# A planned first stage on one core: scores on eight small array tiles, values times rows on two row tiles, and the weight conversion's clip and low word on another engine

## The chip, the cores and the metric

The kernel runs on one core of one Trainium2 chip. The core has a matmul engine (PE, with its weight loads shown as PEld), a vector engine (DVE), an activation engine (ACT), a general engine (POOL) and a queue engine that issues transfers (SP). The metric is device microseconds of one execution; lower is better.

## The reference, cut to what matters

Three blocks follow one another. The first is an attention over a small memory: the rows of `phi` (32 memory slots) are turned into weights `a`, keys and values are pooled with them, and each query attends to the 32 pooled keys.

```python
a = exp(phi - max(phi, axis=2)); a = a / (sum(a, axis=2) + 1e-9)   # b h s m, m = 32
k_m = einsum('bhsm,bhsd->bhmd', a, k); v_m = einsum('bhsm,bhsd->bhmd', a, v)
scores = (1 / sqrt(64)) * q @ k_m.T                                # b h s m
attn = softmax(scores); attn_out = attn @ v_m                      # b h s d
x = attn_out.transpose(0, 2, 1, 3).reshape(8, 576, 512)
h = relu(x.T @ w_tok1) @ w_tok2; u = x + h.T                       # mixes the 576 tokens
x = u + relu(u @ w_ch1) @ w_ch2                                    # 1536 hidden channels
```

The third block is a causal attention with four experts and a top-2 gate. Batch is 8, heads 8, sequence 576, head dimension 64. The weights of the token and channel blocks come as float64.

## The kernel before

Accuracy comes from splitting operands into a high part in a one-pass format (F32R) and a low remainder; a product of two such pairs is three matmuls (`mm3`, L199). Plain F32 matmuls stand in the trace as two records each.

The kernel has three stages. The first, which all of the change is in, goes through 16 units; a unit is one batch and four of its heads (`units`, L296). Unit `n` runs `front(n)` (softmax of `phi` over the sequence, pooled keys and values, queries transposed), `rows(n)` (scores, softmax over the 32 slots, and the weights turned over) and `mix(n)` (token mixing; its output `u1` goes to HBM). After every second unit two `block(j)` do a part of the channel block (two of its 12 slices of 128 hidden channels) on half a batch each; the last two blocks run after the stage. The stage also turns float64 weights into pairs of F32R words (`convert`, L736): ACT takes the absolute high word (`c_abs`), POOL clips it (`c_clip`, L751), POOL scales the low word (`c_low`, L755), DVE joins them and sets the sign (L759, L762), ACT writes the high part (L767), and the remainder is taken on DVE for weights that are needed at once and on POOL for the ten pieces that are needed after the stage (`c_lo`, L771). There are 19 pieces: five for the token weights, four for the blocks of the stage, and ten with a due time (`chan(i, fc, 90000 + 20000 * c)`, L849).

The order of all instructions of the stage is computed in Python before the kernel is built: every step is handed to a planner (`Plan`, L63) with its engine, an assumed duration in ns, what it reads and writes, and the buffer pool it takes from; `order()` lists the steps engine by engine as the assumed durations let them start, the most urgent first. Each engine then executes its list strictly in that order. The assumed durations of the two POOL steps of a conversion are

```python
add("POOL", 150 + 600 * x, c_clip, ...)                     # x = columns / 512
y = add("POOL", 150 + 600 * x, c_low, ..., take="cy", ...)
```

The scores of a unit are four F32 matmuls with a contraction of 64 (the keys of a pair of heads are held block-wise with zeros, so K is 128 and M is 64), on the left and the right half of the array's columns (L481); two pairs of heads, each with 512 and 64 queries. Values times rows (L608 to L610) contract over the 128 rows of four heads with a masked value tile, three matmuls of 288 columns for each of two channel groups and two halves of the sequence. PSUM has two banks each for `t`, `g`, `s` and `b`.

Of the kernel before, what the change touches and what calls it, by code (L numbers as in the profile page):

```python
# [62 lines left out]
class Plan:  # L63
# [5 lines left out]
    def add(self, eng, ns, fn, reads=(), writes=(), take=None, due=None):  # L69
        t = dict(i=len(self.tasks), eng=eng, ns=ns, fn=fn, take=take, due=due, pre=set(), gives=[], holders=0)  # L70
# [19 lines left out]
    def order(self):  # L90
# [13 lines left out]
        slots = dict(self.pools)  # L104
# [9 lines left out]
        while len(out) < len(ts):  # L114
            for eng, cand in open_.items():
                if free_at[eng] > now:
                    continue
                can = [i for i in cand if ready_at[i] <= now and (ts[i]["take"] is None or slots[ts[i]["take"]] > 0)]
# [7 lines left out]
                if t["take"] is not None:  # L126
                    slots[t["take"]] -= 1
# [13 lines left out]
            while True:  # L141
                if i >= 0:
# [5 lines left out]
                    for o in ts[i]["gives"]:  # L148
                        o["holders"] -= 1
                        if not o["holders"]:  # L150
                            slots[o["take"]] += 1
# [8 lines left out]
def fused_kernel(ctx: ExitStack, tc, q, k, v, phi, w_tok1, w_tok2, w_ch1, w_ch2,  # L160
# [106 lines left out]
    with ExitStack() as sa:  # L267
# [12 lines left out]
        kmask = wa.tile([128, 2, 64], F32, name="kmask")  # L280
        DVE.memset(vmask[:], 0.0)
        DVE.memset(kmask[:], 0.0)
        for h in range(4):
            DVE.memset(vmask[32 * h:32 * h + 32, h, :], 1.0)
            DVE.memset(kmask[32 * h:32 * h + 32, h % 2, :], 1.0)
        NB2 = 2
        phb = [ld.tile([128, 4, 5, M], F32, name=f"phb{i}") for i in range(NB2)]
        qTb = [ld.tile([128, 2, S], F32, name=f"qTb{i}") for i in range(NB2)]
# [3 lines left out]
        qn_ = ld.tile([128, 5, 4, D], F32, name="qn")  # L292
        DVE.memset(kv_[ST:128, :, :, 4, :], 0.0)
        DVE.memset(qn_[ST:128, 4, :, :], 0.0)
# [10 lines left out]
        def psum(name, shape=(128, 512)):  # L305
            return pp.tile(list(shape), F32, name=name, bufs=1 if name == "s" else 2)

        def loads(n):
# [15 lines left out]
            def l_q():  # L324
                src = q[b, hs]
                for j in range(4):
                    SP.dma_start(qn_[:, j, :, :], src[:, 0:SM, :].rearrange("h (p j) d -> p j h d", j=4)[:, j])
                SP.dma_start(qn_[0:ST, 4, :, :], src[:, SM:S, :].rearrange("h p d -> p h d"))
# [4 lines left out]
                        q=lambda: add("SP", (3000, 3200), l_q, writes=["qn"]))  # L333

        def front(n):
# [5 lines left out]
            def top():  # L341
                mx = st["mx"] = wk_.tile([128, 4, M], F32, name="pmx", bufs=1)
                m2 = wk_.tile([128, 4, 2, M], F32, name="pm2", bufs=1)
# [50 lines left out]
            def k_scale():  # L394
# [3 lines left out]
                DVE.reciprocal(r[:], r[:])  # L398
                ks = st["ks"] = wk_.tile([128, 2, 64], F32, name="ks", bufs=1)
                DVE.scalar_tensor_tensor(ks[:], p[:, None, 0:64].to_broadcast([128, 2, 64]), r[:],  # L400
                                         kmask[:], op0=OP.mult, op1=OP.mult)
# [24 lines left out]
            def q_t(i):  # L426
                if i < 2:
                    st["q", i] = psum("t")
                    for j in range(4):
                        PE.transpose(st["q", i][:, 128 * j:128 * j + 128], qn_[:, j, 2 * i:2 * i + 2, :], ident[:])  # L430
                    return
                st["q", 2] = psum("t", (128, 2, 128))
                for pr in range(2):
                    PE.transpose(st["q", 2][:, pr, :], qn_[:, 4, 2 * pr:2 * pr + 2, :], ident[:])

            def q_c(i):
                if i < 2:
                    ACT.activation(qT[:, i, 0:512].rearrange("k (p j) -> k p j", j=4),
                                   st["q", i][:].rearrange("k (j p) -> k p j", j=4), AF.Copy)
                else:  # L440
                    ACT.activation(qT[:, :, 512:S], st["q", 2][:, :, 0:ST], AF.Copy)

            add("DVE", 950, top, reads=[kph], writes=["mx"])
# [12 lines left out]
            c = add("DVE", 640, k_scale, reads=[(n, "g")], writes=["ks", (n, "r")])  # L456
# [6 lines left out]
            add("POOL", 780, lambda: v_mask("vh", "Vh"), reads=["vh"], writes=[("Vh", n % 3)])  # L463
            add("POOL", 780, lambda: v_mask("vl", "Vl"), reads=["vl"], writes=[("Vl", n % 3)])
            for i in range(3):
                a = add("PE", (4, 4, 2)[i] * TR, lambda i=i: q_t(i), reads=["qn"], writes=[(n, "q", i)], take="t")
# [3 lines left out]
        def rows(n):  # L470
# [4 lines left out]
            def score():  # L475
                p = st["s"] = psum("s", (128, S))
# [7 lines left out]
            def turn():  # L484
                st["x"] = wk_.tile([128, NB, M], F32, name="ssb", bufs=1)
                DVE.transpose(st["x"][:].rearrange("p k m -> p (k m)"), st["s"][:])
# [1156 lines left out]
```

## Time and profile before

| | us |
|---|---|
| median of three runs | 1269.46 (1268.49 to 1270.68) |
| the profiled execution, its own time | 1271.36 |
| its span in the profile | 1269.6 |
| PE busy | 1186.2 (93%) |
| DVE / ACT / POOL busy | 803.8 / 603.7 / 518.5 |

Line numbers are those of the kernel before. "Busy" of a group is the time in which at least one of its instructions ran; the mean is that of one instruction. Matmuls are pipelined, so the start-to-start distance of neighbours says what one costs, and its record is longer. "Idle before" names what ended the engine's wait. PEclk is the granted clock as a share of full speed.

### The profile page before, as it was taken

Reading aid. Unit: us, or ns where it says so; the run is one execution under the profiler, and the core shown is the slowest. Engines: PE = TensorE matmul, PEld = TensorE weight load, DVE = VectorE, ACT = ScalarE, POOL = GpSimd, SP = SyncE. Lnnn points to the kernel's source line nnn. Section 1 sums busy time; section 2 is a strip of 40 time slices with the busy share of each in tenths; the row PEclk is TensorE's granted clock in tenths of the full one; section 3 lists DMA queues with packets and bytes.
Section 4 is the critical chain, followed back from the end, with each engine's and each line's share of the span. In section 5 each row is a group of like instructions: output and inputs, shape, how many; then the busy total and the mean of one; then the engine's idle time right before and its main releaser. Section 6 shows DMA issues by size and latency. Waiting matters only on the chain.

```text
span 1269.6 us, 23616 instructions
## 1 busy us (share of the span) xinstructions
PE 1186.2 (93%) x8578; PEld 1088.5 (86%) x8578; DVE 803.8 (63%) x1991; ACT 603.7 (48%) x1575; POOL 518.5 (41%) x630
## 2 busy tenths in 40 slices
PE   5567789999997999999999999999999999999998
PEld 3456678899996888998999988999999999999986
DVE  5677776766447175566756552487767677776763
ACT  2344445444434132322232211477776776776775
POOL 5789973434300021211221043564636365373421
PEclk9887999999998999999999999999999999999999
DMA  9666666565226122023212233422332333323523
GB/s 228 181 184 182 179 177 193 161 172 154 75 102 233 47 100 67 34 67 100 100 34 67 100 109 110 131 83 77 95 87 80 89 102 86 94 69 80 158 74 108
DMA packets 161171, 145.07 MB, mean 114 GB/s; under 512 B 73248, under 2 KB 128800, under 8 KB 161056
## 3 DMA queue, kind: packets, MB, share of 16 engines
q1 hardware_dynamic: 161056, 143.57, 38.2%
q8 instruction: 68, 1.11, 0.4%
q14 instruction: 47, 0.39, 0.1%
HBM read 91.10 MB, written 40.89 MB: 104 GB/s over the span
## 4 chain that ended last, share of the span: by engine, by line
PE 77%; POOL 7%; DVE 7%; issue 3%; ACT 3%; DMA 2%; SPq 1%; DVEq 0%; ACTq 0%; POOLq 0%
PE g L199 21%; PE o L199 15%; PE h L199 14%; PE y L1415 4%; PE b L669 3%; PE b L199 3%; PE s L1306 3%; PE t L1370 2%; POOL cy L755 2%; POOL cm L751 1%; PE s L1328 1%; PE s L481 1%; PE g L612 1%; PE g L613 1%; DMA ub<-u_d 1%
## 5 line engine op out<-in xcount | busy, mean ns | idle before, releaser
L1351 POOL TENSOR_TENSOR a<-a,cf 128x128 f32<-128x128 f32 (+3 forms) x128 | 88.2, 720 | 68.1 <-DVE cf L1343 62.1
L199 PE MATMUL o<-hh,w2h 128*128 128x512 f32 x288 | 109.5, 395 | 3.8 <-ACT hh L915 3.8
L199 PE MATMUL o<-hl,w2h 128*128 128x512 f32 x288 | 112.8, 392 | 0.1
L199 PE MATMUL o<-hh,w2l 128*128 128x512 f32 x288 | 112.4, 390 | 0.0
L923 ACT ACTIVATE hh<-m 128x256 fp32r<-128x256 f32 x96 | 38.9, 415 | 111.1 <-DVE m L994 71.4
L1295 DVE CUSTOM_DVE_ANT_0 ssb<-s,cmask 128x128 f32<-128x128 f32 (+2 forms) x144 | 68.5, 482 | 26.7 <-PE s L1306 18.0
L1308 ACT ACTIVATE a<-ssb,nb 128x128 f32<-128x128 f32 (+3 forms) x128 | 71.4, 558 | 18.0 <-DVE nb L1295 15.0
L971 POOL TENSOR_TENSOR tl<-ub,th 128x512 fp32r<-128x512 f32 x12 | 18.1, 1525 | 136.3 <-ACT th L970 136.3
L956 POOL TENSOR_TENSOR ub<-ub 128x512 f32<-128x512 f32 x6 | 9.8, 1630 | 150.4 <-DVE ul L206 150.4
L924 DVE SCALAR_TENSOR_TENSOR hl<-m,hh 128x256 fp32r<-128x256 f32 x96 | 58.2, 615 | 17.6 <-ACT hh L923 15.5
L1207 POOL TENSOR_TENSOR xl<-p,xh 128x288 fp32r<-128x288 f32 x60 | 47.4, 809 | 52.6 <-ACT xh L1206 52.3
L199 PE MATMUL h<-uh,w1h 128*128 128x512 f32 (+2 forms) x200 | 66.4, 334 | 2.0 <-ACT uh L203 2.0
L199 PEld LDWEIGHTS o<-hh,w2h 128*128 128x128 f32 x288 | 54.4, 190 | 14.3 <-ACT hh L915 4.1
L199 PE MATMUL h<-uh,w1l 128*128 128x512 f32 (+2 forms) x200 | 66.7, 334 | 0.0
L199 PE MATMUL h<-ul,w1h 128*128 128x512 f32 (+2 forms) x200 | 65.9, 334 | 0.0
L199 PE MATMUL g<-xh,qkh 128*128 128x288 f32 x232 | 65.3, 301 | 0.0
L199 PE MATMUL g<-xh,qkl 128*128 128x288 f32 x232 | 63.9, 296 | 0.0
L199 PEld LDWEIGHTS o<-hh,w2l 128*128 128x128 f32 x288 | 54.1, 188 | 11.3
L199 PEld LDWEIGHTS o<-hl,w2h 128*128 128x128 f32 x288 | 54.1, 188 | 9.7 <-DVE hl L924 0.4
L916 DVE SCALAR_TENSOR_TENSOR hl<-h,hh 128x512 fp32r<-128x512 f32 x24 | 16.5, 688 | 70.4 <-ACT hh L915 70.4
L206 DVE TENSOR_TENSOR Bl<-t,Bh 128x512 fp32r<-128x512 f32 (+1 forms) x80 | 50.5, 633 | 13.4 <-ACT Bh L203 12.2
L1422 POOL TENSOR_TENSOR yl<-yt,yh 128x256 fp32r<-128x256 f32 x30 | 22.1, 738 | 85.8 <-ACT yh L1421 75.7
(347 smaller groups left out, 4239.8 us busy)
## 6 DMA issues: line engine op xcount, KB each, us to landing
cst<-in_moe_w_ch_dram SPq DMA_DIRECT2D x24, 512.0 KB, 4.1
u_d<-u SPq DMA_DIRECT2D x32, 288.0 KB, 3.3
p_d<-u SPq DMA_DIRECT2D x16, 576.0 KB, 3.3
ub<-u_d SPq DMA_DIRECT2D x9, 1024.0 KB, 5.3
pb<-p_d SPq DMA_DIRECT2D x36, 256.0 KB, 3.5
x_d<-pb SPq DMA_DIRECT2D x36, 256.0 KB, 2.1
u<-u_d SPq DMA_DIRECT2D x16, 576.0 KB, 4.0
p<-x_d SPq DMA_DIRECT2D x15, 576.0 KB, 4.0
```

The source lines that it names most:

```text
L199: PE.matmul(ps, lhsT=a, rhs=b, start=start and i == 0, stop=stop and i == len(seq) - 1)
L206: DVE.tensor_sub(lo, src, f(hi))
L669: PE.matmul(h1[j, fc, "p"][:], lhsT=w[:, kd, :], rhs=x[:, kd, :], start=(part == 0 and i == 0), stop=(part == 1 and i == KD - 1))
L755: POOL.tensor_scalar(st["y"], st["s"][0:P, 0:n, 0].bitcast(U32), 2.0 ** -29, 7.0, op0=OP.mult, op1=OP.min)
L923: ACT.activation(hh, c, AF.Relu)
L924: DVE.scalar_tensor_tensor(hl, c, 0.0, f(hh), op0=OP.max, op1=OP.subtract)
L1207: POOL.tensor_sub(xl[b][:, c, ss], x_, f(xh[b][:, c, ss]))
L1295: DVE.tensor_tensor_reduce(out=out, in0=p, in1=mask, scale=-scale, scalar=least, op0=OP.add, op1=OP.min, accum_out=acc)
L1306: PE.matmul(p[:, 0:W], lhsT=q_[n][:, 128 * c:128 * c + 128], rhs=kk[n][:, 0:W], start=(i == 0), stop=(i == 1))
L1308: ACT.activation(a[:, aoff[c]:aoff[c] + W], s_[:, 0:W], AF.Exp, scale=-1.0, bias=nb[:, 0:1], accum_out=sm[:, c:c + 1])
L1351: POOL.tensor_mul(x_, x_, cf[:, c:c + 1].to_broadcast([128, W]))
L1415: PE.matmul(p[:, lo:w], lhsT=v_[:, kc, 0, :], rhs=x, start=(i == 0), stop=(i == len(ops) - 1))
```

## The change

Five things are edited, and the planner's model of buffers with them.

1. Scores: pooled keys are no longer masked, but copied to both halves of the partitions; queries are laid out as even and odd ones on the two halves. A unit's scores are eight matmuls of K = 64, M = 32 and 288 columns on eight tiles of the array (four column groups times two row groups), into two PSUM banks of the `g` pool, which has four banks now (`s` is gone). The transposes of scores and weights on DVE are two of 288 columns each instead of one of 576.
2. Queries: two transfers per unit instead of five (runs of 1 KB and 512 B instead of 256 B), and the last 64 rows of a head are four small transposes of 32 rows instead of two of 128.
3. Values times rows: K = 64 on the upper or lower row group, the two channel groups in turn, so that neighbours lie on different row groups and banks; the products with `t2` that stood between them come later, with those of the low part.
4. The key scaling goes from DVE to ACT, without its mask; the maximum of `phi` is one reduction instead of three two-input operations; the sum of `e` is taken by POOL and one matmul from the third unit on instead of the seventh (`NR`).
5. Clip, low word and all remainders of the weight conversion run on DVE; POOL has none of it. Several assumed durations are new.

```diff
-        slots = dict(self.pools)
+        rings = {k: [] for k in self.pools}
+        def room(t):
...
+            ring, size = rings[t["take"]], self.pools[t["take"]]
+            return all(o["holders"] == 0 for o in ring[max(0, len(ring) + t["n"] - 2 * size):len(ring) + t["n"] - size])
...
-        NU, NR, NJ = len(units), 6, 2 * B
+        NU, NR, NJ = len(units), 2, 2 * B
-        plan = Plan(pools=dict(t=2, g=2, s=1, b=2, cst=3, cy=2, cm=2),
+        plan = Plan(pools=dict(t=2, g=4, b=2, cst=3, cy=2, cm=2),
...
-                for j in range(4):
-                    SP.dma_start(qn_[:, j, :, :], src[:, 0:SM, :].rearrange("h (p j) d -> p j h d", j=4)[:, j])
-                SP.dma_start(qn_[0:ST, 4, :, :], src[:, SM:S, :].rearrange("h p d -> p h d"))
+                SP.dma_start(qn_[:].rearrange("p h j d -> p h (j d)"),
+                             src[:, 0:SM, :].rearrange("h (p j) d -> p h (j d)", j=4))
+                SP.dma_start(qe_[:], src[:, SM:S, :].rearrange("h (p j) d -> p h (j d)", j=2))
...
-                DVE.tensor_max(m2[:], ph[:, :, 0:2, :], ph[:, :, 2:4, :])
-                DVE.tensor_max(mx[:], ph[:, :, 4, :], m2[:, :, 0, :])
-                DVE.tensor_max(mx[:], mx[:], m2[:, :, 1, :])
+                DVE.tensor_reduce(mx[:], ph[:].rearrange("p h j m -> p h m j"), axis=AX.X, op=OP.max)
...
-                DVE.scalar_tensor_tensor(ks[:], p[:, None, 0:64].to_broadcast([128, 2, 64]), r[:],
-                                         kmask[:], op0=OP.mult, op1=OP.mult)
+                ACT.activation(ks[:], st["g"][:, None, 0:64].to_broadcast([128, 2, 64]), AF.Copy, scale=st["r"][:])
...
-                for pr in range(2):
-                    PE.transpose(st["q", 2][:, pr, :], qn_[:, 4, 2 * pr:2 * pr + 2, :], ident[:])
+                for h in range(4):
+                    PE.transpose(st["q", 2][:, h, :], qe_[:, h, :], ident[0:32, 0:32])
...
-            add("DVE", 950, top, reads=[kph], writes=["mx"])
+            add("DVE", 1320, top, reads=[kph], writes=["mx"])
...
-                for cs in (slice(0, 512), slice(512, S)):
-                    for pr in range(2):
-                        o = 64 * pr
-                        PE.matmul(p[o:o + 64, cs], lhsT=km[:, o:o + 64], rhs=qT[:, pr, cs],
-                                  start=True, stop=True, tile_position=(0, o))
+                for h in range(4):
+                    for j in range(2):
+                        PE.matmul(st["s"][j][32 * h:32 * h + 32, 0:SH], lhsT=km[64 * j:64 * j + 64, 32 * h:32 * h + 32],
+                                  rhs=qT[64 * j:64 * j + 64, h, :], start=True, stop=True, tile_position=(64 * j, 32 * h))
...
-                DVE.transpose(st["a"][:], st["x"][:].rearrange("p k m -> p (k m)"))
+                for j in range(2):
+                    DVE.transpose(st["a"][:].rearrange("p (i j) -> p j i", j=2)[:, j, :],
+                                  st["x"][:, 9 * j:9 * j + 9, :].rearrange("p k m -> p (k m)"))
...
+                for i, (x, y) in enumerate((("Vh", 0), ("Vl", 0), ("Vh", 1))):
+                    for c in range(2):
+                        o = 64 * c
+                        PE.matmul(pu[c], lhsT=st[x][o:o + 64, 2 * c:2 * c + 2, :].rearrange("p h d -> p (h d)"),
+                                  rhs=X[o:o + 64, y, ss], start=(i == 0), stop=False, tile_position=(o, 0))
...
             def c_clip():
-                POOL.tensor_scalar(st["m"], st["m"], LEAST, MOST, op0=OP.max, op1=OP.min)
+                DVE.tensor_scalar(st["m"], st["m"], LEAST, MOST, op0=OP.max, op1=OP.min)
...
-                POOL.tensor_scalar(st["y"], st["s"][0:P, 0:n, 0].bitcast(U32), 2.0 ** -29, 7.0, op0=OP.mult, op1=OP.min)
+                DVE.tensor_scalar(st["y"], st["s"][0:P, 0:n, 0].bitcast(U32), 2.0 ** -29, 7.0, op0=OP.mult, op1=OP.min)
...
-                eng = DVE if early is None else POOL
-                eng.tensor_sub(st["lo"], st["y"].bitcast(F32), f(st["hi"]))
+                DVE.tensor_sub(st["lo"], st["y"].bitcast(F32), f(st["hi"]))
...
-            add("POOL", 150 + 600 * x, c_clip, reads=[("cm", i)], writes=[("cm", i)], due=due)
-            y = add("POOL", 150 + 600 * x, c_low, reads=[("cs", i), ("cm", i)], writes=[("cy", i)], take="cy", due=due)
+            add("DVE", 110 + 400 * x, c_clip, reads=[("cm", i)], writes=[("cm", i)], due=due)
+            y = add("DVE", 70 + 400 * x, c_low, reads=[("cs", i), ("cm", i)], writes=[("cy", i)], take="cy", due=due)
```

## Rows read from the trace of the kernel before

**Rows 1.** Busy time by stretch; columns: stretch, length, PE, PEld, DVE, ACT, POOL busy, clock, DMA, GB/s.

```profile
20.00:180.00 160.00, 109.57 (x1071) 94.68 (x1071) 114.39 (x202) 69.62 (x157) 140.13 (x106) 0.87 0.67 182
180.00:200.00 20.00, 16.30 (x135) 13.64 (x136) 15.65 (x32) 7.59 (x18) 7.68 (x10) 0.91 0.76 242
200.00:340.00 140.00, 138.49 (x1267) 129.13 (x1266) 91.36 (x202) 65.65 (x161) 52.28 (x68) 1.00 0.51 148
340.00:382.00 42.00, 41.72 (x319) 41.23 (x318) 17.12 (x39) 15.57 (x41) 4.26 (x4) 1.00 0.30 101
382.00:404.00 22.00, 13.65 (x70) 11.20 (x69) 20.16 (x41) 13.87 (x29) 0.00 (x0) 0.94 0.74 263
```

**Rows 2.** Chain that ended last, 20 to 180 us: shares by line.

```profile
by line: POOL cy L755 17.1%; POOL cm L751 11.2%; issue 7.6%; POOL ssb L493 5.0%; POOL aT L539 3.9%; PE s L481 3.4%; DMA cst<-in_moe_w_ch_dram 2.9%; DVE cy L762 2.9%; DVE pmx L345 2.6%; DVE at L509 2.4%; DVE pm L344 2.1%; PE t L514 2.0%; PE 
```

**Rows 3.** Groups of instructions on POOL, 20 to 180 us.

```profile
L755 POOL TENSOR_SCALAR cy<-cst 128x512 int32<-128x512 uint32 x16 | 32.1, 2007 | 1.3
L751 POOL TENSOR_SCALAR cm<-cm 128x512 f32<-128x512 f32 x15 | 31.5, 2102 | 1.7 <-ACT cm L748 0.6
...
L771 POOL TENSOR_TENSOR w1l<-cy,w1h 128x512 fp32r<-128x512 f32 x5 | 7.2, 1436 | 0.2
L771 POOL TENSOR_TENSOR w2l<-cy,w2h 128x512 fp32r<-128x512 f32 x5 | 6.5, 1293 | 0.6 <-ACT w2h L767 0.5
```

**Rows 4.** Groups of instructions on DVE, 20 to 180 us.

```profile
L762 DVE SCALAR_TENSOR_TENSOR cy<-cst,cm 128x512 int32<-128x512 int32 x16 | 16.5, 1030 | 0.2
L759 DVE SCALAR_TENSOR_TENSOR cm<-cm,cy 128x512 int32<-128x512 int32 x16 | 11.5, 719 | 17.8 <-POOL cy L755 17.6
...
L345 DVE TENSOR_TENSOR pmx<-phb,pm 128x128 f32<-128x128 f32 x8 | 6.2, 771 | 0.3
L500 DVE TENSOR_REDUCE ssm<-ssb 128x18 f32<-128x576 f32 x8 | 6.0, 747 | 5.8 <-ACT ssb L496 5.8
...
L344 DVE TENSOR_TENSOR pm<-phb 128x256 f32<-128x256 f32 x8 | 5.0, 624 | 0.0
...
L346 DVE TENSOR_TENSOR pmx<-pmx,pm 128x128 f32<-128x128 f32 x8 | 3.5, 434 | 0.3
...
L400 DVE SCALAR_TENSOR_TENSOR ks<-g,kr,kmask 128x128 f32<-128x128 f32 x7 | 2.5, 351 | 0.2
```

**Rows 5.** Three DVE lines by themselves, 0 to 400 us: least, median, greatest ns.

```profile
L225 DVE TENSOR_SCALAR cm<-cm x6: 384/422/957, 186.4 to 395.0; 128x512 f32<-128x512 f32 x6
...
L228 DVE TENSOR_SCALAR cy<-cst x6: 421/425/1633, 181.8 to 395.3; 128x512 int32<-128x512 uint32 x6
...
L345 DVE TENSOR_TENSOR pmx<-phb,pm x16: 277/294/1266, 7.5 to 284.4; 128x128 f32<-128x128 f32 x16
```

**Rows 6.** Busy time of the 20 us in which DVE is busiest.

```profile
120.00:140.00 20.00, 16.11 (x136) 14.44 (x135) 17.45 (x33) 8.96 (x20) 18.37 (x16) 0.88 0.79 219
```

**Rows 7.** PE in order of time: start, length of the record, instruction.

```profile
215.41 0.28 PE L570 MATMUL g<-t1l,ahi 128*128 128x256 f32 x1
215.62 1.19 PE L481 MATMUL s<-qTb,kmT 128*64 128x512 f32 x8
216.74 0.40 PE L608 MATMUL g<-aT,Vh 128*128 128x288 f32 x1
216.98 0.29 PE L609 MATMUL g<-aT,Vl 128*128 128x288 f32 x1
217.11 0.29 PE L610 MATMUL g<-aT,Vh 128*128 128x288 f32 x1
...
221.34 0.38 PE L434 MATMUL t<-ident,qn 128*128 128x128 f32 x2
```

**Rows 8.** Groups on PE, 200 to 382 us.

```profile
L608 PE MATMUL g<-aT,Vh 128*128 128x288 f32 x43 | 13.9, 322 | 0.9 <-ACT u L623 0.8
...
L481 PE MATMUL s<-qTb,kmT 128*64 128x512 f32 x28 | 7.6, 618 | 0.0
```

**Rows 9.** DMA issues of the queries, 0 to 400 us: count, KB each, us to landing.

```profile
qn<-in_q_dram SPq DMA_DIRECT2D x64, 128.0 KB, 3.0
```

More of the change, by code (lines that the diff above doesn't have):

```diff
@@ L67, in __init__, with add @@
         self.tasks, self.wrote, self.read = [], {}, {}
-    def add(self, eng, ns, fn, reads=(), writes=(), take=None, due=None):
-        t = dict(i=len(self.tasks), eng=eng, ns=ns, fn=fn, take=take, due=due, pre=set(), gives=[], holders=0)
+    def add(self, eng, ns, fn, reads=(), writes=(), take=None, n=1, due=None):
+        t = dict(i=len(self.tasks), eng=eng, ns=ns, fn=fn, take=take, n=n, due=due, pre=set(), gives=[], holders=0)
         for k in reads:
@@ L117, in order @@
                     continue
-                can = [i for i in cand if ready_at[i] <= now and (ts[i]["take"] is None or slots[ts[i]["take"]] > 0)]
+                can = [i for i in cand if ready_at[i] <= now and room(ts[i])]
                 if not can:
@@ L126, in order @@
                 if t["take"] is not None:
-                    slots[t["take"]] -= 1
+                    rings[t["take"]] += [t] * t["n"]
                 if eng == "SP":
@@ L279, in fused_kernel @@
         vmask = wa.tile([128, 4, 64], F32, name="vmask")
-        kmask = wa.tile([128, 2, 64], F32, name="kmask")
         DVE.memset(vmask[:], 0.0)
-        DVE.memset(kmask[:], 0.0)
         for h in range(4):
             DVE.memset(vmask[32 * h:32 * h + 32, h, :], 1.0)
-            DVE.memset(kmask[32 * h:32 * h + 32, h % 2, :], 1.0)
         NB2 = 2
         phb = [ld.tile([128, 4, 5, M], F32, name=f"phb{i}") for i in range(NB2)]
-        qTb = [ld.tile([128, 2, S], F32, name=f"qTb{i}") for i in range(NB2)]
+        qTb = [ld.tile([128, 4, SH], F32, name=f"qTb{i}") for i in range(NB2)]
         for i in range(NB2):
@@ L305, in psum @@
         def psum(name, shape=(128, 512)):
-            return pp.tile(list(shape), F32, name=name, bufs=1 if name == "s" else 2)
+            return pp.tile(list(shape), F32, name=name, bufs=4 if name == "g" else 2)
         def loads(n):
@@ L455, in front @@
                 add("PE", 130, kv_sum, reads=["es"], writes=[(n, "g")])
-            c = add("DVE", 640, k_scale, reads=[(n, "g")], writes=["ks", (n, "r")])
+            add("DVE", 330, k_scale, reads=[(n, "g")], writes=[(n, "r")])
+            c = add("ACT", 315, k_mul, reads=[(n, "g"), (n, "r")], writes=["ks"])
             d = add("ACT", 315, v_scale, reads=[(n, "g"), (n, "r")], writes=["vm"])
@@ L539, in xlo @@
                 POOL.tensor_sub(st["X"][:, 1, :], st["a"][:], f(st["X"][:, 0, :]))
[L541 to L542 removed]
+            a = add("PE", 650, score, reads=[kkm, (*kqT, 0), (*kqT, 1), (*kqT, 2)], writes=[(n, "s")], take="g", n=2)
+            c = add("DVE", 840, lambda: (turn(0), turn(1)), reads=[(n, "s")], writes=["x"])
             free(a, c)
             add("DVE", 755, most, reads=["x"], writes=["smx"])
[L545 removed]
+            add("POOL", 1230, sub, reads=["smx", "x"], writes=["x"])
             add("ACT", 690, exp, reads=["x"], writes=["x"])
             add("DVE", 1150, total, reads=["x"], writes=[(n, "sm")])
[L548 to L549 removed]
+            add("POOL", 1240, scaled, reads=[(n, "sm"), "x"], writes=["x"])
+            add("DVE", 840, back, reads=["x"], writes=["a"])
             a4 = add("PE", 4 * TR, to_rows, reads=["a"], writes=[(n, "p4")], take="t")
@@ L617, in u_b @@
                 for t in range(2):
-                    PE.matmul(st["u", c, hf], lhsT=st["hl"][:, t, cs], rhs=t2h[:, t, ss], start=False, stop=(t == 1))
+                    PE.matmul(st["u", hf][c], lhsT=st["hh"][:, t, cs], rhs=t2h[:, t, ss], start=False, stop=False)
+                    PE.matmul(st["u", hf][c], lhsT=st["hh"][:, t, cs], rhs=t2l[:, t, ss], start=False, stop=False)
+                for t in range(2):
+                    PE.matmul(st["u", hf][c], lhsT=st["hl"][:, t, cs], rhs=t2h[:, t, ss], start=False, stop=(t == 1))
             def u_c(c, hf):
-                if g == 0 and c == 0 and hf == 0:
+                if b not in u1:
                     u1[b] = wk1.tile([128, KD, S], F32, name="u1", bufs=2)
-                ACT.activation(u1[b][:, 2 * g + c, SH * hf:SH * hf + SH], st["u", c, hf], AF.Copy)
+                ACT.activation(u1[b][:, 2 * g + c, SH * hf:SH * hf + SH], st["u", hf][c], AF.Copy)
             def u_s(c):
@@ L782, in convert @@
             h_ = add("ACT", 110 + 520 * x, c_hi, reads=[("cy", i)], writes=[("ch", i)], due=due)
-            if early is None:
-                l_ = add("DVE", 110 + 580 * x, c_lo, reads=[("cy", i), ("ch", i)], writes=[key], due=due)
-            else:
-                l_ = add("POOL", 150 + 1150 * x, c_lo, reads=[("cy", i), ("ch", i)], writes=[key], due=due)
+            l_ = add("DVE", 110 + 580 * x, c_lo, reads=[("cy", i), ("ch", i)], writes=[key], due=due)
             free(y, h_, l_)
```

81 lines of the change are left out of this document (37 added, 44 removed).

## Prediction

> **What bounds the kernel now.** Read the busy time by stretch first [rows 1]. The stage that the change is in ends near 382 us, and it has two halves with different limits. From 200 to 382 us PE is busy for 180.2 of 182 us at full clock: here only work taken off PE counts. From 20 to 180 us PE is busy for 109.6 of 160 us at a clock of 0.87, DVE for 114.4, and POOL for 140.1, which is 88%. The second view is the chain that ended last in that stretch [rows 2]: clip and low word of the weight conversion, both on POOL, are 28% of it, the largest two lines. The third is the groups on POOL [rows 3]: each of these two takes 2.0 to 2.1 us on 512 columns, where the planner assumed 750 ns. So the lists were made for a POOL that is nearly three times as fast as it is, and the steps behind each conversion on POOL's list (the softmax of the scores, the value splits) are late by the difference. I read the front as bound by POOL. After 382 us PE has a hole of 8 us while DVE is busy for 20.2 of 22 us [rows 1]; nothing of the change is there, and all that follows moves with the end of the stage, unchanged.
>
> **POOL's relief.** The 31 clips and low words of 512 columns take 63.6 us of POOL, the ten remainders 13.7 us [rows 3]; six more of other widths, one of them of 256 columns, are some 10 us at the same rate. POOL keeps 140 - 87 = 53 us of the 160. The sum of `e` comes to it for four more units: three two-input operations each, at most at the 1.44 us of a remainder [rows 3], so at most 17 us. POOL then stands at 33 to 44%; I take 40%. It bounds the front no more, and the question is what does.
>
> **What DVE gets.** The same clip and low word, done on DVE elsewhere in this kernel, take 0.42 us each (medians) [rows 5], a fifth of POOL's time: 38 of them are 16.1 us. Ten remainders at the 0.72 us of the two-input join on 512 columns [rows 4] are 7.2 us. DVE does not always get its time undisturbed: the median of the second maximum of `phi` is 0.29 us [rows 5], but its mean is 0.77 us in the front [rows 4], and clip and low word reach 0.96 and 1.63 us [rows 5]. That is a wait of 0.48 us on average beside a POOL that is 88% busy; at 40% I scale it to 0.22 us, 10.5 us for 48 instructions. The Trainium skill (SBUF — State Buffer, Who interferes with whom) says that DVE and GpSimd share a pair of ports and that a `tensor_scalar` which runs in a two-port mode locks the other out for a whole instruction; the spread of these rows agrees with that.
>
> DVE gives up: three maxima of 0.62 + 0.77 + 0.43 us for one reduction. A reduction of 576 columns takes 0.75 us [rows 4], so 640 are 0.83 us if the strided order costs nothing; the change assumes 1.32 us; I take 1.0 us, 0.83 us less for each of eight units, 6.6 us. The masked key scaling is 2.5 us [rows 4]. The sign step takes 1.03 us where the join of the same shape takes 0.72 us [rows 4]; with POOL calmer I take 3 of these 5 us. So DVE's work of the front is 114.4 + 16.1 + 7.2 + 10.5 - 6.6 - 2.5 - 3 = 136 us.
>
> **The front.** The greatest share that DVE reaches over 20 us in the stage is 17.45 of 20, 87% [rows 6]. With all ten late pieces (the ones with due times) still in the front, 136 / 0.87 = 156 us instead of 160: 4 us won. But they are the least urgent work on DVE's list, and with DVE's load now stated about right they can wait for the second half, where DVE is busy for 91 of 140 us [rows 1]. One takes 0.42 + 0.42 + 0.72 + 0.8 + 0.72 = 3.1 us of DVE. Without any of them the front is (136 - 31) / 0.87 = 121 us, 39 won. I take half of them: 120.5 / 0.87 = 138 us, **22 us** won. From 180 to 200 us PE is busy for 16.3 of 20 [rows 1]; blocks that come earlier fill half of that hole: **2 us**. At the head the queries need two issues instead of five ahead of `phi`, keys and values, and their transfers of 128 KB land after 3.0 us [rows 9]; one of 512 KB lands later than the first of these did. I take **2 us** won, between 0 and 4.
>
> **PE's own work, from 200 us on.** A unit's scores run from 215.62 to the next start at 216.74, 1.12 us for 576 columns on two halves of the array [rows 7]. Afterwards each of the eight tiles streams 288. If all run together that is 0.56 us; if the two row groups take turns, 1.12 us and nothing is won. Matmuls on two row groups at once show in no row. I take 0.65 us, nearer to the first, since the two groups share neither array rows nor banks. The Trainium skill (TensorE: Matmul & The Clock Gate, Measured speedup vs the span model) gives some 4 ns for each further tile that runs beside the first; by that an estimate is 0.59 us, and the sum would be 0.4 us better. Seven units are scored in this half (28 records, two for each of two pairs) [rows 8]: 3.3 us won.
>
> Values times rows are six matmuls per half of the sequence at a pace of 0.13 us (216.98 to 217.11) [rows 7], 0.8 us. As pairs they are 0.4 us, but entering and leaving a tiled group costs extra: the scores begin 0.21 us after the matmul before them instead of 0.12, and the second matmul behind them comes after 0.24 us instead of 0.13 [rows 7]. With 0.2 us for that a half takes 0.6 us, and with eleven units (43 records of four each, one missing) [rows 8] 2 x 0.2 x 11 = 4.4 us are won. Taking turns, it would be 4.4 us lost. The four small transposes instead of two (0.38 us for the pair [rows 7]) cost between 0 and 0.38 us; at 0.1 us and seven units 0.7 us. Together **7 us** won, between 13 won and 7 lost.
>
> Costed at nothing: the key scaling on ACT (ACT is busy for 69.6 of 160 us in the front [rows 1]; if it were full, 0.3 us a unit), the split transposes on DVE (same columns; some 0.06 us a unit), the sums of `e` (POOL's new slack hides them; PE saves a little). The products with `t2` that now wait for the low part `hl` too have other blocks' matmuls to hide behind; in the second half PE waited for almost nothing [rows 8].
>
> **Sum.** 22 + 2 + 2 + 7 = 33 us: 1271.4 - 33 = 1238 us for an execution like the profiled one. That one is 1.9 us above the median of the runs, so I forecast **1236 us**.
>
> **Rivals.**
>
> *The row groups take turns.* No row shows them together. Then PE loses 7 instead of winning 7: 1236 + 14 = 1250 us. For it: the trace has column groups only.
>
> *DVE takes POOL's place.* The late pieces stay in the front; it shrinks by 4 us, the head by 2, PE gives 7: 1269.5 - 13 = 1256 us or a little more. For it: the list is greedy and runs unurgent work early, as POOL's list did (the ten remainders all lie ahead of 180 us [rows 3]). Against it: a step that takes 0.4 us holds up little.
>
> *Slower: the shared port.* Each of the 38 new instructions waits 0.48 us as the maxima did, and nothing is relieved: 114.4 + 16.1 + 7.2 + 48 x 0.48 = 161 us of DVE, 185 us at 87%, 25 us lost, 9 won elsewhere: 1285 us. It decides as soon as DVE's work in the front passes 0.87 x 160 = 139 us, only 3 us above my sum with all the pieces, so the late pieces' place matters. Speaking for it: the greatest times in [rows 5]. By the skill's rule above it is the engine that issues first that holds the pair, so DVE would block POOL as well. Against it: POOL loses more than half of its work.
>
> *All late pieces slip,* and PE fills the front: 39 instead of 22 us, 1219 us, some 10 less if the clock recovers too.
>
> **How the numbers follow.** Forecast (1218 to 1248) 0.54; row groups in turn 0.12; DVE instead of POOL 0.14, of which 0.04 within no change; slower 0.11; all slip 0.09. This kernel's runs tell 0.2% (2.5 us) from no change. Faster 0.85, same 0.04, slower 0.11. The range reaches from the last case to a little past the DVE case, **1207 to 1262 us**; it leaves out the slower case and the edges.
>
> **What would show it.** Right: POOL below 50% in the front, clip and low word near 0.42 us on DVE, the first block's matmuls ahead of 100 us, the stage's end near 350 us, scores of 0.65 us and pairs of value matmuls starting together; the part after the stage as long as before (887 us). Wrong: DVE over 87% in the front with PE waiting for it, or the eight score tiles in turn.

## The result and the profile after

The change takes 1215.95 us (median of 4 executions, 1215.17 to 1219.02) against 1269.03 us (4 executions, 1268.49 to 1270.68): a ratio of 0.9584, interval 0.9564 to 0.9604. That is 53 us won where 33 were forecast, inside the range. The profiled execution took 1216.71 us with a span of 1215.0 us.

The windows of the kernel after answer to [rows 1]; the columns are the same. The last output of the stage (`u`, L629 here) starts at 332.9 us instead of 382.2.

```profile
20.00:180.00 160.00, 145.97 (x1450) 124.60 (x1458) 154.36 (x294) 93.65 (x217) 79.47 (x93) 0.95 0.77 228
180.00:200.00 20.00, 18.03 (x180) 16.08 (x174) 18.97 (x37) 9.73 (x21) 8.01 (x8) 1.00 0.37 118
200.00:340.00 140.00, 132.14 (x1185) 121.00 (x1184) 86.45 (x192) 67.36 (x165) 37.23 (x48) 0.99 0.47 149
0.00:333.00 333.00, 301.34 (x2895) 264.40 (x2896) 263.42 (x530) 172.39 (x403) 128.80 (x160) 0.97 0.63 189
333.00:352.00 19.00, 15.49 (x77) 13.81 (x76) 16.65 (x34) 10.43 (x22) 0.00 (x0) 0.82 0.87 301
```

The same stage of the kernel before, in one window:

```profile
0.00:382.00 382.00, 317.16 (x2893) 285.35 (x2894) 246.53 (x503) 164.51 (x385) 209.18 (x196) 0.94 0.59 166
```

The gain lies where it was forecast: in the front, from 20 to 180 us, PE is busy for 146 us instead of 110. Over the whole stage PE's busy time fell by 16 us (317 to 301, at a granted clock of 0.97 instead of 0.94) and its idle time by 33 (382 - 317 = 65 to 333 - 301 = 32). What follows the stage is nearly as long as before: 1215.0 - 332.9 = 882 us against 1269.6 - 382.2 = 887. But DVE in the front is at 154 of 160 us, 96%, far above the 87% that the prediction took for its limit. PE does not wait for it more than before: from 20 to 180 us its waits for DVE are 31 us in the kernel before and 9 us here. The longest of each, before and after (us in total, times, longest):

```profile
PE t L514 <- DVE at L509: 12.7, 3, 7.9
...
PE t L349 <- DVE pmx L345: 4.7, 1, 4.7
```

The chain that ended last from 20 to 180 us has no longer a line that leads, though most of its larger lines are DVE's; the two POOL lines that were 28% of it [rows 2] are gone:

```profile
by line: DVE cy L763 5.7%; DVE ul L668 5.4%; issue 5.1%; DVE cy L770 5.1%; DVE cm L767 5.0%; DVE pmx L345 4.5%; DVE cm L759 3.9%; DVE ssm L503 3.8%; PE b L204 3.4%; DVE ssb L489 3.4%; PE g L380 3.3%; DVE at L513 3.1%; DVE smx L493 2.9%; PE 
```

The groups on DVE in the front answer to [rows 4], those of L763 and L759 to [rows 3]:

```profile
L345 DVE TENSOR_REDUCE pmx<-phb 128x128 f32<-128x640 f32 x10 | 12.9, 1292 | 0.0
L763 DVE TENSOR_SCALAR cy<-cst 128x512 int32<-128x512 uint32 x15 | 11.8, 792 | 0.0
L759 DVE TENSOR_SCALAR cm<-cm 128x512 f32<-128x512 f32 x13 | 7.6, 587 | 0.0
L778 DVE TENSOR_TENSOR w2l<-cy,w2h 128x512 fp32r<-128x512 f32 x6 | 7.3, 1211 | 0.0
L778 DVE TENSOR_TENSOR w1l<-cy,w1h 128x512 fp32r<-128x512 f32 x6 | 7.0, 1169 | 0.0
```

The same two steps as lines by themselves, over the stage (least, median, greatest ns; first and last start):

```profile
L759 DVE TENSOR_SCALAR cm<-cm x19: 396/437/1497, 15.6 to 192.9; 128x512 f32<-128x512 f32 x16, 128x576 f32<-128x576 f32 x2, 128x256 f32<-128x256 f32 x1
...
L763 DVE TENSOR_SCALAR cy<-cst x19: 378/428/1654, 18.9 to 194.3; 128x512 int32<-128x512 uint32 x16, 128x576 int32<-128x576 uint32 x2, 128x256 int32<-128x256 uint32 x1
```

All 19 pieces still start ahead of 195 us. No late piece slipped into the second half, from 200 us on: half of them doing so was where the prediction's largest term came from. The last pieces do come later than before, though the stage is shorter: the last clip started at 166.5 us in the kernel before and starts at 192.9 here.

PE in order of time, around one half of a sequence of values times rows and around one unit's scores, answers to [rows 7]:

```profile
224.49 0.27 PE L575 MATMUL g<-t1l,ahi 128*128 128x256 f32 x1
224.69 0.40 PE L615 MATMUL g<-aT,Vh 64*128 64x288 f32 x2
224.93 0.30 PE L615 MATMUL g<-aT,Vl 64*128 64x288 f32 x2
225.06 0.29 PE L615 MATMUL g<-aT,Vh 64*128 64x288 f32 x2
225.28 0.39 PE L580 MATMUL g<-t1h,alo 128*128 128x256 f32 x1
...
244.13 0.71 PE L483 MATMUL g<-qTb,kmT 64*32 64x288 f32 x16
244.78 0.40 PE L677 MATMUL b<-uh,w1h 128*128 128x288 f32 x1
```

The eight score tiles hold PE for 244.78 - 244.13 = 0.65 us, the six value matmuls for 225.28 - 224.69 = 0.59 us, in pairs (two records in one line) with 0.13 us between the second and the third. These are the forecast 0.65 and 0.6.

### The profile page after: what moved, and what is told of

It reads as the page before. It is cut to its first block, busy times and chain, and to the rows that moved or that the text cites. A ratio compares the mean times of both kernels' runs of the same rounds, so it can differ in the third digit from the quotient of the medians.

```text
span 1215.0 us, 23518 instructions
## 1 busy us (share of the span) xinstructions
PE 1170.2 (96%) x8586; PEld 1068.1 (88%) x8586; DVE 821.8 (68%) x2017; ACT 611.7 (50%) x1591; POOL 438.7 (36%) x594
## 4 chain that ended last, share of the span: by engine, by line
PE 77%; DVE 13%; ACT 2%; issue 2%; DMA 2%; POOL 2%; SPq 0%; DVEq 0%; ACTq 0%; POOLq 0%
PE g L204 22%; PE o L204 15%; PE h L204 15%; PE y L1419 4%; PE b L204 3%; PE s L1310 3%; PE t L1374 3%; PE b L677 3%; DVE ul L668 2%; PE s L1332 1%; PE g L621 1%; PE g L380 1%; DMA ub<-u_d 1%; PE g L615 1%; POOL a L1355 1%
## 5 line engine op out<-in xcount | busy, mean ns | idle before, releaser
L1312 ACT ACTIVATE a<-ssb,nb 128x128 f32<-128x128 f32 (+3 forms) x128 | 71.3, 558 | 18.4 <-DVE nb L1299 15.1
L919 ACT ACTIVATE hh<-h 128x512 fp32r<-128x512 f32 x24 | 14.3, 595 | 76.7 <-PE h L204 76.7
```

The costliest lines, as they stand in the source:

```text
L1312: ACT.activation(a[:, aoff[c]:aoff[c] + W], s_[:, 0:W], AF.Exp, scale=-1.0, bias=nb[:, 0:1], accum_out=sm[:, c:c + 1])
```

## The experiments

Two theories of the front stood against each other. **Amount:** POOL had too much to do, and taking the conversion off it is the gain (the prediction's). **Order:** POOL's list was made with 750 ns for steps that take 2.0 us, so urgent steps stand behind conversions; lists made with the right durations bring the gain on any engine. Ratios are to the kernel before on the same chip, each with its 95% interval. Where an edit changes what a step costs, the planner's assumed duration changes with it, so each of these kernels has lists of its own.

### The conversion by itself, and its durations by themselves

`conv_alone`: the kernel before with clip, low word and all remainders on DVE, with DVE's durations; nothing else of the change.

```diff
-                POOL.tensor_scalar(st["m"], st["m"], LEAST, MOST, op0=OP.max, op1=OP.min)
+                DVE.tensor_scalar(st["m"], st["m"], LEAST, MOST, op0=OP.max, op1=OP.min)
...
-            add("POOL", 150 + 600 * x, c_clip, reads=[("cm", i)], writes=[("cm", i)], due=due)
+            add("DVE", 110 + 400 * x, c_clip, reads=[("cm", i)], writes=[("cm", i)], due=due)
```

> The kernel before with the weight conversion's clip, low word and late remainders on DVE, nothing else changed. If POOL's relief is the cause of most of the gain: 30 to 40 us faster than before (1230 to 1240 us), DVE above 90% busy between 20 and 180 us. If the smaller work on PE is the cause: under 12 us faster (1257 us or more). If the wrong assumed durations of POOL are the cause, this gains as in the first case, and the third kernel of this group gains as much.

`pool_true_cost`: the kernel before with two numbers of the planner changed. Every instruction stays on its engine; only the order of the lists is another.

```diff
-            add("POOL", 150 + 600 * x, c_clip, reads=[("cm", i)], writes=[("cm", i)], due=due)
-            y = add("POOL", 150 + 600 * x, c_low, reads=[("cs", i), ("cm", i)], writes=[("cy", i)], take="cy", due=due)
+            add("POOL", 150 + 1900 * x, c_clip, reads=[("cm", i)], writes=[("cm", i)], due=due)
+            y = add("POOL", 150 + 1850 * x, c_low, reads=[("cs", i), ("cm", i)], writes=[("cy", i)], take="cy", due=due)
```

> The kernel before, the lists made with 2.05 and 2.0 us for clip and low word on POOL, all instructions and engines as they were. If the lists were the fault: 20 us or more faster, because urgent steps no longer stand behind conversions. If POOL's plain amount of work is the fault: within 6 us of before, since POOL still has 140 us to do.

Measured: `conv_alone` 1240.47 us, 0.9764 (0.9744 to 0.9785). `pool_true_cost` 1243.66 us, 0.9791 (0.9770 to 0.9811): the two intervals overlap. The first is half a us outside the range that both theories had named (1230 to 1240 us), the second is what order alone had (20 us or more faster). The front of `pool_true_cost`, and its clip as a line by itself:

```profile
20.00:180.00 160.00, 132.67 (x1288) 114.35 (x1291) 126.31 (x232) 79.42 (x180) 134.72 (x109) 0.88 0.73 202
...
L751 POOL TENSOR_SCALAR cm<-cm x19: 1562/1921/2745, 15.4 to 195.5; 128x512 f32<-128x512 f32 x16, 128x576 f32<-128x576 f32 x2, 128x256 f32<-128x256 f32 x1
```

The clip takes 1.92 us, hardly less than before (2.01, both medians), POOL is still busy for 134.72 of 160 us (84%, against 88%), and the clock is as low (0.88 against 0.87 [rows 1]). Yet PE gets 133 us of work into the stretch instead of 110, and the stage ends at 357.4 us. The conversions give way: the last clip starts at 195.5 us instead of 166.5. The waits show what the order had cost. In the kernel before, 20 to 180 us (us in total, times, longest):

```profile
DVE cm L759 <- POOL cy L755: 21.1, 13, 3.5
ACT ssb L496 <- POOL ssb L493: 18.8, 8, 4.1
```

The second is the softmax of the scores: ACT's exponential waits for the subtraction of the maxima on POOL. POOL in order of time shows why, in the kernel before:

```profile
66.95 2.43 POOL L751 TENSOR_SCALAR cm<-cm 128x512 f32<-128x512 f32 x1
69.46 1.94 POOL L755 TENSOR_SCALAR cy<-cst 128x512 int32<-128x512 uint32 x1
71.48 1.66 POOL L493 TENSOR_TENSOR ssb<-ssb,smx 128x576 f32<-128x576 f32 x1
```

The maxima that L493 needs were ready at 66.03 + 0.74 = 66.77 us, by DVE in order of time:

```profile
66.03 0.74 DVE L490 TENSOR_REDUCE smx<-ssb 128x18 f32<-128x576 f32 x1
```

The planner had the conversion's two steps done in 1.5 us; they took 4.4, and the subtraction began 71.48 - 66.77 = 4.7 us after its input was ready. In `pool_true_cost` the maxima are ready at 67.15 + 0.74 = 67.89 us and the subtraction begins 0.35 us later, without a conversion between:

```profile
67.15 0.74 DVE L490 TENSOR_REDUCE smx<-ssb 128x18 f32<-128x576 f32 x1
...
68.24 1.27 POOL L493 TENSOR_TENSOR ssb<-ssb,smx 128x576 f32<-128x576 f32 x1
```

Over the front, the first of the two waits is no longer among the 23 largest there, and the second has shrunk from 18.8 us in 8 times to:

```profile
ACT ssb L496 <- POOL ssb L493: 4.3, 5, 1.4
```

So most of what moving the conversion brings, 26 of 30 us, comes without moving it. Order holds; amount as the bound of the front falls. The counterpart, the conversion on DVE with durations as wrong as POOL's, was not run.

### The conversion undone in the kernel after

`conv_back`: after, with the conversion (late remainders too) back on POOL and its old durations. `conv_back_true`: the same with the right ones. The clip's line in each of the two:

```diff
-            add("DVE", 110 + 400 * x, c_clip, reads=[("cm", i)], writes=[("cm", i)], due=due)
+            add("POOL", 150 + 600 * x, c_clip, reads=[("cm", i)], writes=[("cm", i)], due=due)     # conv_back
+            add("POOL", 150 + 1900 * x, c_clip, reads=[("cm", i)], writes=[("cm", i)], due=due)    # conv_back_true
```

> The changed kernel with the whole conversion back on POOL as before, with the assumed 750 ns. If POOL's relief is the cause: 1245 to 1260 us, POOL again above 80% between 20 and 180 us. If PE's smaller work is the cause: 1225 to 1235 us.

> The changed kernel with the conversion on POOL, but with assumed durations of 2.05 and 2.0 us. Theory now (the lists: the wrong 750 ns put urgent steps behind conversions on POOL): 1214 to 1224 us, as fast as the changed kernel or nearly, with POOL still above 75% busy between 20 and 180 us. Rival (the move to DVE itself is worth some 25 us): 1235 to 1242 us, as with the wrong durations.

Measured: `conv_back` 1241.25 us, 0.9773 (0.9752 to 0.9794); `conv_back_true` 1220.20 us, 0.9618 (0.9603 to 0.9632). The first lies between the ranges of its two theories (1245 to 1260 and 1225 to 1235 us), the second in that of order. In the presence of the other edits the durations are worth 0.9773 - 0.9618 = 0.0155, 20 us, and the engine 0.9618 - 0.9584 = 0.0034, 4 us, with intervals that touch. In `conv_back` the front also had the lower clock, 0.85 against 0.91 in `conv_back_true`; what of the 20 us is the clock's was not separated. The front of `conv_back_true` has POOL busier than it was before, at 142.59 of 160 us:

```profile
20.00:180.00 160.00, 139.23 (x1405) 118.70 (x1404) 127.36 (x241) 90.49 (x210) 142.59 (x124) 0.91 0.72 214
```

DVE is at 127 us there instead of 154, and the stage ends at 333.7 us, no earlier than with the change.

`late_rem_pool`: after, with only the ten late remainders back on POOL. If DVE at 96% were the bound, this relief would help.

```diff
-                DVE.tensor_sub(st["lo"], st["y"].bitcast(F32), f(st["hi"]))
+                eng = DVE if early is None else POOL
+                eng.tensor_sub(st["lo"], st["y"].bitcast(F32), f(st["hi"]))
```

> The changed kernel with only the ten late remainders back on POOL, which is half idle now. If DVE's 96% between 20 and 180 us is the bound: 4 to 10 us faster, since 11 us leave DVE. If the order of urgent steps is all that counts and late work sits in gaps: within 3 us.

Measured: 1222.25 us, 0.9633 (0.9617 to 0.9649), some 6 us slower than the change, which neither theory had. The stage itself ends no later, at 332.1 us against 332.9; the loss lies in what follows it, 1218.7 - 332.1 = 886.6 us against 882.1, and why is open. DVE did not become emptier, other work took the place, so this run does not settle what a lighter DVE would bring:

```profile
20.00:180.00 160.00, 139.92 (x1431) 117.77 (x1432) 157.22 (x293) 93.59 (x216) 91.24 (x102) 0.95 0.77 231
```

### PE's part

`values_full_rows`: after, values times rows as full-array matmuls again. `pe_part_undone`: that, and all eight score tiles on one row group, so that the odd queries' scores are computed from the even operands.

```diff
-                        PE.matmul(pu[c], lhsT=st[x][o:o + 64, 2 * c:2 * c + 2, :].rearrange("p h d -> p (h d)"),
-                                  rhs=X[o:o + 64, y, ss], start=(i == 0), stop=False, tile_position=(o, 0))
+                        PE.matmul(pu[c], lhsT=st[x][:, 2 * c:2 * c + 2, :].rearrange("p h d -> p (h d)"),
+                                  rhs=X[:, y, ss], start=(i == 0), stop=False)
...
-                                  rhs=qT[64 * j:64 * j + 64, h, :], start=True, stop=True, tile_position=(64 * j, 32 * h))
+                                  rhs=qT[0:64, h, :], start=True, stop=True, tile_position=(0, 32 * h))
```

> The changed kernel with values times rows on the full array again (K = 128, no row tiles), in the new order. By the prediction's term (0.4 us a unit on PE) at most 6.4 us slower, 3 to 6 us as PE is busy nearly everywhere; if row tiles were worth their full half (0.8 us a unit) 10 to 13 us slower; if they bring nothing, within 2 us.

> The changed kernel with values times rows on the full array, and the scores' two row groups put on one (the odd queries' scores are computed from the even queries' operands, so the output isn't the reference's), so that they run in turn. If PE's smaller work is what the rest of the gain comes from: 10 to 15 us slower than the changed kernel (0.4 + 0.5 us on each of 16 units). If DVE or data set the pace where PE had gaps: under 5 us slower.

Measured: 1215.49 us, 0.9575 (0.9548 to 0.9602), and 1218.12 us, 0.9600 (0.9583 to 0.9618). The first is the change's own time, the second's interval overlaps with it. PE in `values_full_rows`, where the six take 242.32 - 241.53 = 0.79 us in some halves and 270.17 - 269.29 = 0.88 us in others:

```profile
241.40 0.30 PE L677 MATMUL b<-uh,w1l 128*128 128x288 f32 x1
241.53 0.43 PE L615 MATMUL g<-aT,Vh 128*128 128x288 f32 x2
...
242.32 0.52 PE L580 MATMUL g<-t1h,alo 128*128 128x256 f32 x3
...
269.29 0.51 PE L615 MATMUL g<-aT,Vh 128*128 128x288 f32 x2
269.64 0.43 PE L615 MATMUL g<-aT,Vl 128*128 128x288 f32 x2
269.90 0.43 PE L615 MATMUL g<-aT,Vh 128*128 128x288 f32 x2
270.17 0.30 PE L677 MATMUL b<-uh,w1h 128*128 128x288 f32 x1
```

PE in `pe_part_undone`, where a unit's scores take 257.38 - 256.25 = 1.13 us:

```profile
256.25 1.19 PE L483 MATMUL g<-qTb,kmT 64*32 64x288 f32 x16
257.38 0.40 PE L677 MATMUL b<-uh,w1h 128*128 128x288 f32 x1
```

So the tiles do what they should: 1.13 - 0.65 = 0.48 us a unit on the scores and 2 x (0.79 to 0.88, less 0.59) = 0.4 to 0.58 on the values, at most 14 to 17 us of PE over 16 units. In part it is less, since the tiled values begin 224.69 - 224.49 = 0.20 us after the matmul ahead of them and the full-array ones 241.53 - 241.40 = 0.13. Given back, the tiles cost 0 to 2 us, less than the intervals are wide. That is not because PE has room in the second half. These are `after` and `pe_part_undone` from 200 us to the end of the stage:

```profile
200.00:332.90 132.90, 128.55 (x1162) 117.63 (x1161) 80.27 (x178) 62.74 (x154) 37.23 (x48) 1.00 0.44 141
...
200.00:332.30 132.30, 131.98 (x1172) 125.38 (x1171) 73.54 (x168) 60.89 (x148) 39.41 (x51) 1.00 0.37 121
```

Without the tiles PE is full there, and the stage ends no later. Where the rest of the work given back went was not resolved.

### The planner's buffers, the banks, the queries, the small edits

`free_any_buffer`: after, with the old rule that a step may take a buffer when any one of its pool is free, instead of the one next in turn.

```diff
-            return all(o["holders"] == 0 for o in ring[max(0, len(ring) + t["n"] - 2 * size):len(ring) + t["n"] - size])
+            return sum(o["holders"] > 0 for o in rings[t["take"]]) + t["n"] <= self.pools[t["take"]]
```

> The changed kernel with the old model of buffers in its planner (a step may start when enough buffers of its pool are free, whichever they are). If the model of buffers is where the other 20 to 25 us come from: 1230 us or more. If it is not: within 5 us of the changed kernel.

`banks_split`: after, with the scores in a pool of two banks of their own and two left for `g`, instead of four that all share.

```diff
-        plan = Plan(pools=dict(t=2, g=4, b=2, cst=3, cy=2, cm=2),
+        plan = Plan(pools=dict(t=2, g=2, s=2, b=2, cst=3, cy=2, cm=2),
...
-                st["s"] = [psum("g") for _ in range(2)]
+                st["s"] = [psum("s") for _ in range(2)]
```

> The changed kernel with two banks for the scores alone and two for all else of the g pool, instead of four shared ones. If the shared banks are what lets the lists run ahead: 10 us or more slower. If the banks don't matter: within 4 us.

`lists_alone`: before, with the new rule for buffers, the right conversion durations of `pool_true_cost` and the durations of five other steps on POOL that the change corrects.

```diff
-            add("POOL", 780, lambda: v_mask("vh", "Vh"), reads=["vh"], writes=[("Vh", n % 3)])
+            add("POOL", 900, lambda: v_mask("vh", "Vh"), reads=["vh"], writes=[("Vh", n % 3)])
...
-            add("POOL", 1200, xlo, reads=["a", ("X", n % 2)], writes=[("Xl", n % 2)])
+            add("POOL", 1540, xlo, reads=["a", ("X", n % 2)], writes=[("Xl", n % 2)])
```

> The kernel before with only its lists made anew: the changed kernel's model of buffers (in turn, not any free one), 2.05 and 2.0 us for clip and low word on POOL, and the changed kernel's durations for POOL's other steps. No instruction, engine or buffer is changed. If the lists are the whole matter: 1217 to 1228 us, near the changed kernel. If the rest of the gain needs the other edits (four shared banks, fewer or other instructions): 1238 to 1246 us, as with POOL's two durations alone.

`q_small_runs`: after, with the 512 main queries of each head loaded by four transfers of 256-byte runs again (and a longer assumed duration for them).

```diff
-                SP.dma_start(qn_[:].rearrange("p h j d -> p h (j d)"),
-                             src[:, 0:SM, :].rearrange("h (p j) d -> p h (j d)", j=4))
+                for j in range(4):
+                    SP.dma_start(qn_[:, :, j, :], src[:, 0:SM, :].rearrange("h (p j) d -> p j h d", j=4)[:, j])
```

> The changed kernel with the queries loaded in four transfers of 256-byte runs again, to the same places. If the transfers matter for the rest of the gain: 8 us or more slower. If they are hidden, as the prediction had it, within 3 us.

`small_edits_undone`: after, with three maxima of `phi` in place of one reduction, and the sum of `e` on POOL from the seventh unit on, as before.

```diff
-        NU, NR, NJ = len(units), 2, 2 * B
+        NU, NR, NJ = len(units), 6, 2 * B
...
-                DVE.tensor_reduce(mx[:], ph[:].rearrange("p h j m -> p h m j"), axis=AX.X, op=OP.max)
+                DVE.tensor_max(m2[:], ph[:, :, 0:2, :], ph[:, :, 2:4, :])
+                DVE.tensor_max(mx[:], ph[:, :, 4, :], m2[:, :, 0, :])
+                DVE.tensor_max(mx[:], mx[:], m2[:, :, 1, :])
```

> The changed kernel with three maxima on DVE instead of the one reduction, and the sum of e taken by PE for six units instead of two. If these small edits carry part of the rest: 5 us or more slower. If not: within 3 us; a little faster is possible, since three undisturbed maxima are 1.0 us and the reduction 1.29 us.

| kernel | us | ratio (95%) | end of the stage, us | from there to the end of the span, us |
|---|---|---|---|---|
| after | 1215.95 | 0.9584 (0.9564 to 0.9604) | 332.9 | 882.1 |
| free_any_buffer | 1225.84 | 0.9658 (0.9641 to 0.9675) | 336.7 | 887.0 |
| banks_split | 1231.68 | 0.9704 (0.9688 to 0.9720) | 347.1 | 881.3 |
| lists_alone | 1249.01 | 0.9840 (0.9825 to 0.9854) | 363.4 | 885.6 |
| q_small_runs | 1217.72 | 0.9596 (0.9582 to 0.9611) | 328.2 | 886.6 |
| small_edits_undone | 1210.49 | 0.9531 (0.9517 to 0.9546) | 329.8 | 879.7 |

The four shared banks are worth 0.9704 - 0.9584, 15 us, and the rule for buffers 0.9658 - 0.9584, 9 us; the queries' transfers 2 us, within the interval. The last column, from the profiled executions, says where: of the rule's 9 us only 4 lie in the stage, and the front of `free_any_buffer` had a clock of 0.88 instead of 0.95; the 15 us of the banks lie in the stage. Why the part behind the stage varies by some 7 us was not resolved. The rule for buffers lies between the two answers expected (1230 us or more, within 5 us of the change). `banks_split` has PE less busy in the front, 139 us instead of 146:

```profile
20.00:180.00 160.00, 138.61 (x1330) 116.71 (x1331) 153.11 (x282) 90.48 (x206) 72.81 (x84) 0.94 0.73 214
```

Which steps the two pools held up was not resolved further. `lists_alone` was slower than `pool_true_cost` (0.9840 against 0.9791) and than either range expected of it, although its planner knows more: on the old banks the better rule, or the five longer durations, made a worse list. Which of the two did is open. It also says how far a difference can be trusted: any new duration makes another list, and lists differ by 6 us here without an instruction changed. The 26 and 20 us of the durations are far beyond that; differences of a few us may be the luck of a list.

`small_edits_undone` is the fastest of all, 0.0053 or 7 us better than the change by the ratios, with intervals that do not meet (its upper end is 0.9546, the lower end of the change 0.9564). It beats both kernels, and by more than the 3 us expected at most; 3 us lie in the stage. The three maxima in its front:

```profile
L346 DVE TENSOR_TENSOR pm<-phb 128x256 f32<-128x256 f32 x10 | 7.0, 705 | 0.0
L347 DVE TENSOR_TENSOR pmx<-phb,pm 128x128 f32<-128x128 f32 x10 | 6.0, 595 | 0.3
L348 DVE TENSOR_TENSOR pmx<-pmx,pm 128x128 f32<-128x128 f32 x10 | 4.9, 488 | 0.3
```

and what the change put on POOL for the sum of `e`, for each unit, in the kernel after:

```profile
L371 POOL TENSOR_TENSOR es<-ea 128x256 f32<-128x256 f32 x9 | 8.7, 971 | 4.9 <-ACT ea L365 4.7
L372 POOL TENSOR_TENSOR es<-ea,es 128x128 f32<-128x128 f32 x9 | 5.5, 615 | 0.7
L373 POOL TENSOR_TENSOR es<-es,es 128x128 f32<-128x128 f32 x9 | 5.5, 612 | 0.7
```

These are 0.97 + 0.62 + 0.61 = 2.2 us between the exponential and the pooling of a unit. The three maxima take 0.71 + 0.60 + 0.49 = 1.8 us on average, more than the 1.29 us of the one reduction, so DVE's time in this step does not explain the gain; the sum of `e` is the likelier part. The two edits were undone together, so this is argued and not shown.

## Why the prediction was right, and where it was wrong

The direction and the range held, and so did the place: the front. The size did not, 53 us instead of 33, and the reason behind the largest term was another. That the time fell into the range is in part luck: what carried it there has no term in the sum.

**The step that failed** is "I read the front as bound by POOL", with the sum that followed from it: POOL's load off, DVE's load on, divided by the 87% of [rows 6]. POOL's 88% was busy time, not a bound. With 84% (`pool_true_cost`) the stage ended 25 us earlier, with 89% and the other edits (`conv_back_true`) 48.5 us earlier. The prediction had the real cause in hand, "the lists were made for a POOL that is nearly three times as fast as it is", but priced the load and not the lists.

**DVE at 87%.** The prediction took the greatest share in [rows 6] for what DVE can reach, and "DVE over 87%" for a sign of trouble. It went to 96% with the stage 49 us shorter. The 87% was what the old lists let DVE reach, not a limit of the engine. The front is full now for another reason as well: ten units' scores start in it, seven before.

**The late pieces.** Half of the ten were to slip and bring 22 us; none did (the last starts at 192.9 us). The front's 22 us became 30 for the conversion (`conv_alone`) without that mechanism.

**What was missing.** The four shared banks (15 us) and the planner's rule for buffers (9 us) have no term in the sum. `conv_alone` and the whole change are 0.9764 - 0.9584 apart, 23 us; these two edits, 24 us, are of that size. Against them stand the reduction and the earlier sum of `e`, which cost 7 us where the sum had them as a small gain. The undoings are not additive, and part of the rule's 9 us lies behind the stage, so the division is rough.

**PE's work.** Right in price (0.65 and 0.59 us for 0.65 and 0.6), wrong in worth: 7 us were counted from a second half where PE was full. Given back, the tiles cost 0 to 2 us, though PE is full there without them; what makes up for them was not resolved. By the Trainium skill (TensorE: Matmul & The Clock Gate, Measured speedup vs the span model) an estimate for the scores was 0.59 us, which the row exceeds by 0.06.

**DVE's terms.** Clip and low word: 0.42 us and 0.22 of waiting forecast; medians 0.437 and 0.428, with means of 0.587 and 0.792 the waiting is 0.15 and 0.36. The remainders, at 0.72 + 0.22, took 1.17 to 1.21. The reduction of `phi`: 1.0 taken, 1.29 measured, near the upper bound of 1.32 that the change itself assumes. The sum added 136 - 114 = 22 us to DVE in the front; over the whole stage, where the later units' savings count too, DVE got 263 - 247 = 17 us more. So the load was priced about right, and dividing it by 87% was not.

**The small terms.** Of the hole from 180 to 200 us PE fills 18.03 instead of 16.30 us, the 2 us forecast; the first unit's scores start at 15.1 us instead of 16.8, near the 2 us for the head.

**The signs.** POOL at 79.47 / 160 = 49.7% (the sum took 40%), the first block's matmul at 75.9 us instead of 108.6, the scores and the pairs came as named; the stage's end at 332.9 was earlier than "near 350". Of the first sign of being wrong one half came, DVE over 87%; the other, PE waiting for it, did not: its waits for DVE fell from 31 to 9 us in the front.

**The rivals.** Row groups in turn: fell, 0.65 against 1.13 us on one row group. DVE in POOL's place: DVE leads the chain, but the front did not stay long; whether a lighter DVE would shorten it further was not shown. The shared port: waits are there, yet DVE passed the 139 us at which it was to decide and the time fell. All late pieces slip, 1219 us, is nearest to the time and did not happen: no piece slipped. The clock that it counted on rose from 0.87 to 0.95 in the front, but hardly in `pool_true_cost` (0.88), so most of its 26 us cannot come from it. What the clock gave to the 53 us was not separated.

## What to carry to other kernels

Where each engine follows a list that was made ahead, a high busy share is by itself no bound: first compare the durations that the list was made with to those in the trace, correct them, and only then move work. Cost the rules of the planner and the sharing of banks like instructions, by an experiment that changes them alone. And work saved on an engine that is full in one stretch is not by that worth its time: undo it in the changed kernel and measure.

## What the runs showed of the hardware

A maximum over five strided elements, 640 inputs to 128 results, takes 1.29 us, while sums over 32 contiguous ones, 576 inputs to 18 results, took 0.75 us [rows 4]. Whether the stride or the many short groups cost the difference was not separated. The clip, 16 times of 19 on 512 columns, takes 1.92 us on POOL (median of `pool_true_cost`) and 0.437 on DVE, 4.4 times less. Eight 64x32 tiles run together in 0.65 us, and in 1.13 on one row group. A group of value tiles costs PE something at its edges: six half-height matmuls take 0.59 us where three at a pace of 0.13 us would be 0.4.
